# Key products of the next batch behind the last totals of the current one, value turning in front of the first query products

## The chip, the cores and the metric

The kernel runs on one core of a Trainium2 chip. The metric is the device time of one execution in microseconds (us), as the median of several runs. Beside it stands one profiled execution, whose span runs from its first to its last instruction. The engines are TensorE (PE, with its weight loads listed apart as PEld), VectorE (DVE), ScalarE (ACT), GpSimd (POOL) and SyncE (SP, whose queue issues most DMAs).

## The reference

Two stages follow each other. The first is a linear attention with a degree-two sketch; the second is a gated feed-forward block (FFN) over the result.

```python
q, k, v: (4, 4, 1088, 32)       # batch, heads, sequence, head size;  S1, S2: (8, 32)
phi(x)  = outer(S1 x, S2 x)      # 8 x 8 = 64 features for each position
kv  = sum_s phi(k)_s v_s         # 64 x 32 for each batch and head
z   = sum_s phi(k)_s             # 64
out = (phi(q) kv) / (phi(q) z + 1e-6)
x   = out as (4352, 128)         # positions x (heads * head size)
y   = (silu(x w_gate) * (x w_val)) w_out     # d_ff = 1536
```

## The kernel before

Everything is fp32. The 4352 positions are cut into 12 blocks, three for each batch, of 384, 384 and 320 positions (`steps`, `blocks`). The FFN works on one block and one of 12 slices of d_ff at a time. `unit(i, j)` (L519 to L535) does two 128x128 matmuls into two PSUM banks, g and u, then a Silu on ScalarE from g, then on VectorE the product `hj` with u. `down()` (L547) multiplies an earlier `hj` with `wo` and sums twelve of them in the bank `acc`. With the twelfth, `store` turns the block back on VectorE (L575) and issues four output DMAs on SP. `down` runs two units behind (`LAG`). Three PSUM banks, g0 to g2, serve g and u in turn through `bank()`, so g of a unit takes the bank that u of two units earlier had, and waits for that unit's `hj`. The sums of a new block wait in the same way for L575 of the block before.

The attention of batch b+1 is spread over the FFN of batch b. `attention(b)` is a generator; each `next` runs it up to its next `yield`, and the piece's instructions are put behind the unit and the `down` just written. The lists `groups` say behind which units that is. Engines work their instructions in the order written (`manual_schedule`), so this order is the schedule. The pieces of one batch are:

- `turn_k` twice (L260): VectorE transposes the loaded keys `kld` into `kT`; then `load_k(b + 1)` refills `kld` over SP.
- key products (L276): 18 matmuls in two pieces of chunks, (0, 5) into the PSUM tile a and (5, 9) into the tile b. Behind each piece ScalarE copies half of the products to `ka` (L290). `key_features` (L296) then multiplies on VectorE, and `feature_sums` adds up on GpSimd (L453).
- values and sums (L307, L477), 40 matmuls into a, and their copy (L481); `load_v(b + 1)`; the turning of the first queries (L266).
- `turn_kv` (L330): four matmuls that turn values and sums into b, copied to `kvz` on ScalarE (L490).
- three times: query products (L351) into a and b, ScalarE copies `qb` (L365), VectorE products `phq` (L379); then, in a piece of its own, totals (L401) into a or b and `divide` (L422 to L447), five VectorE instructions that write the block's `xT`.

The tiles a and b are two PSUM banks wide each. The attention matmuls use small parts of the array (L276 and L330 128 rows by 64 columns, L307 and L477 128 by 32, L351 32 by 64, L401 64 by 32), while the FFN uses all of it.

The first batch's attention is computed in a start-up stage written out by hand. Then come the FFN units of batch 0, in an order written out (`seq`), with the first pieces of `attention(1)` among the last of them. After these follows a stretch without units, called the drain below: groups of three leftover `down`s alternate with pieces of `attention(1)`. Then the loop at L749 runs batches 1 to 3 with 36 units each, z = 0 to 35; in batches 1 and 2 the pieces of the next attention stand behind the units named in `groups`. Each piece between two FFN matmuls is called an attention group below.

Of the kernel before, what the change touches and what calls it, by code (L numbers as in the profile page):

```python
# [17 lines left out]
def kernel(  # L18
# [29 lines left out]
    P = nc.NUM_PARTITIONS  # L48
    B, H, S, Dh = q.shape
# [5 lines left out]
    NC = (NX + 3) // 4  # L55
# [9 lines left out]
    steps = [(sum(plan[:s]), n) for s, n in enumerate(plan)]  # L65
# [20 lines left out]
    def bank(tag=None):  # L86
        if tag is None:
            tag = free_banks[turn[0] % len(free_banks)]
            turn[0] += 1
        return psum.tile([P, TB], FP32, tag=tag, name="bank")  # L90

    def wide(tag):
        return psum.tile([P, 2, TB], FP32, tag=tag, name=tag)
# [17 lines left out]
    kpieces = ((0, 5), (5, NC))  # L111
# [3 lines left out]
    def load_k(b):  # L115
        nc.sync.dma_start(
            out=kld[:, 0:NX, :], in_=k[b].rearrange("h (pp x) d -> (h pp) x d", pp=32)
        )

    def load_q(b, x0=0, x1=NX):  # L120
        src = q[b].rearrange("h (pp x) d -> (h pp) x d", pp=32)
        nc.sync.dma_start(out=qld[:, x0:x1, :], in_=src[:, x0:x1, :])
# [124 lines left out]
    def run(*gens):  # L247
        for g in gens:
            for _ in g:
                pass  # L250
# [7 lines left out]
    def turn_k(c0, c1):  # L258
        four = "p (a c) d -> p a c d"
        nc.vector.transpose(  # L260
            out=kT[:, c0:c1, :, :].rearrange("p c a t -> p a c t"),
            in_=kld[:].rearrange(four, a=4)[:, :, c0:c1, :],
        )
# [7 lines left out]
    def key_products(ps, c0, c1, aside=False):  # L271


        for c in range(c0, c1):
            for a in (0, 2):
                nc.tensor.matmul(  # L276
                    ps[32 * a : 32 * a + 64, 64 * (c - c0) : 64 * (c - c0) + 64],
                    kT[:, c, a : a + 2, :].rearrange("p a t -> p (a t)"),
                    s12[:].rearrange("p h t r -> p (h t r)"),
                    start=True,  # L280
                    stop=True,
                )
        n = c1 - c0
        ab = ps[:, 0 : 64 * n].rearrange("p (x t r) -> p x t r", t=2, r=R)
        if aside:
            kab = apool.tile([P, n * H, 2, R], FP32, tag="kab", name="kab")
            nc.scalar.copy(kab[:], ab)
            return kab[:, :, 0, :], kab[:, :, 1, :]
        ka = apool.tile([P, n * H, R], FP32, tag="ka%d" % c0, name="ka")
        nc.scalar.copy(ka[:], ab[:, :, 0, :])  # L290
        return ka[:], ab[:, :, 1, :]
# [102 lines left out]
    def totals(n, phq, kvz, nd):  # L394

        w = 32 * n
        for t in (1, 0):
            for h in range(H):
                for half in range(2):
                    r = slice(F * half, F * half + F)  # L400
                    nc.tensor.matmul(  # L401
                        halves(nd[t])[half][32 * h : 32 * h + 32, 0:w],
                        kvz[t][r, 32 * h : 32 * h + 32],
                        phq[r, h, 0:w],
                        start=True,
                        stop=True,
                    )
        return nd

    def side_by_side(tag):  # L410
        both = wide(tag)[:].rearrange("p g (t w) -> p g t w", t=2)
        return both[:, :, 0, :], both[:, :, 1, :]

    def divide(b, x0, n, nd, among=()):


        w = 32 * n
        t0 = S * b + 64 * x0
        dT = apool.tile([P, 2 * XS, 32], FP32, tag="dT", name="dT", bufs=2)
        rc = apool.tile([P, 2 * XS], FP32, tag="rc", name="rc", bufs=2)  # L420
        rd = apool.tile([P, 2 * XS, 32], FP32, tag="rd", name="rd", bufs=2)
        nc.vector.transpose(  # L422
            out=dT[:, 0 : 2 * n, :].rearrange("p (a x) t -> p a x t", a=2),
            in_=nd[1][:, :, 0:w].rearrange("p a (x t) -> p a x t", t=32),
        )
        nc.vector.tensor_scalar_add(rc[:, 0 : 2 * n], dT[:, 0 : 2 * n, 0], 1e-6)
        nc.vector.reciprocal(rc[:, 0 : 2 * n], rc[:, 0 : 2 * n])
        nc.vector.transpose(
            out=rd[:, 0 : 2 * n, :], in_=rc[:, 0 : 2 * n].unsqueeze(2).to_broadcast([P, 2 * n, 32])
        )  # L430
        if among:
            part(*among)
        xs = xT[:, t0 : t0 + 2 * w].rearrange("p (x a t) -> p a x t", a=2, t=32)
        rs = rd[:, 0 : 2 * n, :].rearrange("p (a x) t -> p a x t", a=2)
        flat, deep = "p (x t) -> p x t", "p a (x t) -> p a x t"
        if isinstance(nd[0], list):
            todo = [(xs[:, a], nd[0][a][:, 0:w].rearrange(flat, t=32), rs[:, a]) for a in (0, 1)]
        else:
            todo = [(xs, nd[0][:, :, 0:w].rearrange(deep, t=32), rs)]
        if t0 == blocks[LAST][0]:  # L440

            m = SPLIT // 64
            ys = xT[:, t0 + SPLIT : t0 + BW].rearrange("p (t x a) -> p a x t", a=2, t=32)
            _, num, r = todo.pop()
            todo = [(xs[:, :, 0:m], num[:, :, 0:m], r[:, :, 0:m]), (ys, num[:, :, m:], r[:, :, m:])]
        for x, num, r in todo:
            nc.vector.tensor_tensor(out=x, in0=num, in1=r, op=ALU.mult)  # L447
# [9 lines left out]
        add(s[:, 0, :], s[:, 0, :], rows[:, 8, :])  # L457
        return s[:, 0, :].rearrange("p (h f) -> p h f", h=H)

    def attention(b):  # L460

        for c0, c1 in kpieces:
            turn_k(c0, c1)
            if c1 == NC and b + 1 < B:
                load_k(b + 1)
            yield
        phk = apool.tile([P, NC, H, R, R], FP32, tag="phk", name="phk")
        prods = [key_products(wide(t)[:, 0, :], *c) for t, c in zip("ab", kpieces)]
        key_features(phk, prods[0], *kpieces[0])
        yield  # L470
        key_features(phk, prods[1], *kpieces[1])
        zs = feature_sums(phk)
        yield
        kvp = wide("a")
        key_values(kvp[:, 0, :], phk, 0, NC)
        for h in range(H):
            nc.tensor.matmul(  # L477
                kvp[32 * h : 32 * h + 32, 1, 0:F], ones[:], zs[:, h, :], start=True, stop=True
            )
        kvs = apool.tile([P, 2, F], FP32, tag="kvs", name="kvs")  # L480
        nc.scalar.copy(kvs[:], kvp[:, :, 0:F])  # L481
        if b + 1 < B:
            load_v(b + 1, [nc.sync] * 4)
        turn_q(*steps[0])
        yield
        kvz = apool.tile([P, 2, P], FP32, tag="kvz", name="kvz", bufs=2)
        kzp = wide("b")[:, 0, 0 : 2 * P].rearrange("p (t n) -> p t n", t=2)
        for t in range(2):
            turn_kv(kvs[:, t, :], kzp[:, t, :])
        nc.scalar.copy(kvz[:], kzp)  # L490
        kvz = kvz[:, 0, :], kvz[:, 1, :]
        yield
        tags = "ab"
        for i, (x0, n) in enumerate(steps):
            phq = query_features(n, query_products(x0, n, tags))
            if i + 1 < len(steps):
                turn_q(*steps[i + 1])
            elif b + 1 < B:
                load_q(b + 1)
            yield  # L500
            divide(b, x0, n, totals(n, phq, kvz, side_by_side(tags[0])))
            tags = tags[::-1]
            yield


# [113 lines left out]
    for c in fpieces:  # L619
        turn_k(*c)  # L620
    prods = [
        key_products(bank(t), *c, aside=(c[1] == NC))
        for t, c in zip(("g1", "g2", "acc"), fpieces)
    ]
    phk = apool.tile([P, NC, H, R, R], FP32, tag="phk", name="phk")
    kz, kv = bank("g0")[:, 0 : H * F], wide("b")[:, 0, 0:F]
    n = steps[0][1]
# [13 lines left out]
    kvz = [apool.tile([P, P], FP32, name=x) for x in ("kvz0", "kvz1")]  # L641
# [5 lines left out]
    phq = query_features(n, pss, qbs)  # L647
# [17 lines left out]
    nd = totals(n, phq, kvz, ([bank(t) for t in ("g2", "acc")], side_by_side("a")[0]))  # L665
# [8 lines left out]
    att = attention(1)  # L674
# [4 lines left out]
    phq = query_features(steps[1][1], pss, qbs)  # L679
# [40 lines left out]
    for z, (i, j) in enumerate(seq):  # L720
# [15 lines left out]
        if z in groups:  # L736
            next(att)
    todo.sort()
    while todo:
        for _ in range(3):  # L740
            if todo:
                down()
        next(att, None)
    run(att)

    groups = (0, 1, 3, 4, 8, 11, 14, 17, 20, 23, 26, 29)
    for b in range(1, B):  # L749
        att = attention(b + 1) if b + 1 < B else None  # L750
        for z in range(3 * NCH):
            i, j = z // NCH, z % NCH
            unit(3 * b + ((0, 2, 1)[i] if b == B - 1 else i), j)
            for _ in range(2):
                if len(todo) > LAG:
                    down()
            if att and z in groups:
                next(att)
        if att:
            run(att)  # L760
    ps = wide("a")[:, 0, 0:D]
    for j in range(NCH):
        if todo and j % 4 == 0:
# [39 lines left out]
```

## Time and profile before

| what | value |
|---|---|
| median of 3 runs | 321.84 us (321.78 to 322.18) |
| the profiled execution's own time | 321.65 us |
| its span | 319.9 us |
| TensorE clock granted | 0.999 |
| PE busy | 312.2 us, 98% of the span |
| VectorE busy | 157.8 us, 49% |
| ScalarE busy | 99.0 us, 31% |
| GpSimd busy | 37.6 us, 12% |

The page counts busy time over the whole span. A matmul's end is modelled and its start is recorded, so the distances between starts tell more than the busy time. In an answer of the timeline a row gives the start, the time from the first start to the last end, the engine, the line, the operation with the names of its tiles, the shapes, and a count; an fp32 matmul appears there as two passes, so "x2" is one matmul.

### The profile page before, as it was taken

The numbers are of one execution on the slowest core, as the hardware profiler recorded it, in microseconds if no ns is written. First come the engines' busy times: TensorE is split into PE (matmuls) and PEld (weight loads), VectorE is DVE, ScalarE is ACT, GpSimd is POOL, SyncE is SP. The second block draws the span as 40 slices with busy tenths as digits, with TensorE's granted clock in tenths as the row PEclk, the third lists the DMA queues.
The fourth block names the chain that finished last, engine by engine and source line by source line (L and its number), as shares of the span: only waits on it lengthen the run. The fifth ranks groups of instructions, "written<-read, shape, count | busy, mean of one in ns | idle before, by whom it ended". The sixth has DMA issues, their size and how long they took to land.

```text
span 319.9 us, 5604 instructions
## 1 busy us (share of the span) xinstructions
PE 312.2 (98%) x2300; PEld 193.7 (61%) x2300; DVE 157.8 (49%) x332; ACT 99.0 (31%) x227; POOL 37.6 (12%) x53
## 2 busy tenths in 40 slices
PE   8989999999999999999999999999999999999994
PEld 6545565655556665555666656555667655676664
DVE  4887999442556532554643542354544332323321
ACT  3467755321211322222322222313222222222230
POOL 2324234072000230000000060000000000000000
PEclk9999999999999999999999999999999999999999
DMA  7553490204041201100210100100010100100101
GB/s 206 155 151 100 162 243 2 72 0 97 2 94 27 65 22 50 27 0 2 39 58 0 22 2 0 24 4 2 0 27 0 21 0 2 26 0 0 21 2 25
DMA packets 24665, 13.99 MB, mean 44 GB/s; under 512 B 18368, under 2 KB 22720, under 8 KB 24640
## 3 DMA queue, kind: packets, MB, share of 16 engines
q1 hardware_dynamic: 24000, 13.54, 16.7%
q8 instruction: 18, 0.29, 0.4%
q10 hardware_dynamic: 640, 0.10, 0.2%
q14 instruction: 7, 0.06, 0.1%
HBM read 11.41 MB, written 2.23 MB: 43 GB/s over the span
## 4 chain that ended last, share of the span: by engine, by line
PE 88%; DVE 7%; issue 2%; ACT 1%; POOL 0%; DVEq 0%
PE bank L519 49%; PE bank L547 27%; DVE hj L533 2%; PE a L351 2%; PE a L401 2%; PE b L351 1%; PE bank L197 1%; PE a L307 1%; DVE exp L227 1%; PE a L561 1%; DVE man L231 1%; PE b L401 1%; PE a L276 1%; DVE exp L219 1%; ACT exp L224 1%
## 5 line engine op out<-in xcount | busy, mean ns | idle before, releaser
L533 DVE TENSOR_TENSOR hj<-sg,bank 128x384 f32<-128x384 f32 (+1 forms) x138 | 72.7, 528 | 118.2 <-PE bank L519 117.3
L525 ACT ACTIVATE sg<-bank 128x384 f32<-128x384 f32 (+1 forms) x144 | 67.9, 472 | 162.7 <-PE bank L519 161.9
L519 PE MATMUL bank<-xT,wg 128*128 128x384 f32 (+1 forms) x288 | 113.7, 477 | 1.2 <-POOL wg L235 1.1
L519 PE MATMUL bank<-xT,wv 128*128 128x384 f32 (+1 forms) x288 | 111.5, 469 | 0.5 <-DVE hj L533 0.5
L547 PE MATMUL bank<-hj,wo 128*128 128x384 f32 (+2 forms) x288 | 106.8, 462 | 0.3 <-DVE hj L533 0.2
L519 PEld LDWEIGHTS bank<-xT,wv 128*128 128x128 f32 x288 | 54.4, 190 | 34.5 <-DVE hj L533 2.1
L547 PEld LDWEIGHTS bank<-hj,wo 128*128 128x128 f32 x288 | 53.9, 190 | 33.2 <-issue 2.4
L519 PEld LDWEIGHTS bank<-xT,wg 128*128 128x128 f32 x288 | 52.7, 190 | 32.3 <-issue 3.9
L453 POOL TENSOR_TENSOR zs<-phk 128x1024 f32<-128x1024 f32 x3 | 7.0, 2348 | 115.5 <-PE bank L519 106.0
L379 DVE TENSOR_TENSOR phq<-a,qb 128x384 f32<-128x384 f32 (+1 forms) x11 | 5.8, 531 | 10.7 <-ACT qb L365 10.7
L365 ACT COPY qb<-a 128x384 f32<-128x384 f32 (+1 forms) x11 | 5.1, 460 | 15.1 <-PE b L351 8.6
L351 PE MATMUL a<-qT,sq 32*64 32x192 f32 (+1 forms) x176 | 9.2, 324 | 0.0
L351 PE MATMUL b<-qT,sq 32*64 32x192 f32 (+1 forms) x176 | 9.2, 324 | 0.0
L227 DVE SCALAR_TENSOR_TENSOR exp<-raw,exp 128x384 int32<-128x384 int32 (+2 forms) x14 | 8.6, 618 | 0.9 <-ACT exp L224 0.9
L224 ACT ACTIVATE exp<-exp,rebias 128x384 int32<-128x384 int32 (+3 forms) x15 | 8.2, 550 | 2.7 <-DVE exp L219 2.0
L422 DVE STREAM_TRANSPOSE dT<-a 128x384 f32<-128x384 f32 (+1 forms) x8 | 4.4, 550 | 7.8 <-PE a L401 7.8
L365 ACT COPY qb<-b 128x384 f32<-128x384 f32 (+1 forms) x11 | 5.1, 463 | 9.7 <-PE b L351 6.4
L575 DVE STREAM_TRANSPOSE o<-bank 128x384 f32<-128x384 f32 (+2 forms) x12 | 6.6, 549 | 2.7 <-PE bank L547 2.3
L351 PEld LDWEIGHTS a<-qT,sq 32*64 32x64 f32 x176 | 5.5, 131 | 3.9 <-issue 3.0
L379 DVE TENSOR_TENSOR phq<-b,qb 128x384 f32<-128x384 f32 (+1 forms) x11 | 5.8, 527 | 4.2 <-ACT qb L365 4.2
L231 DVE SCALAR_TENSOR_TENSOR man<-raw,man 128x384 f32<-128x384 uint32 (+2 forms) x14 | 6.9, 493 | 0.0
L225 ACT ACTIVATE man<-man 128x384 f32<-128x384 int32 (+3 forms) x15 | 6.7, 450 | 0.5 <-DVE man L220 0.5
(96 smaller groups left out, 168.9 us busy)
## 6 DMA issues: line engine op xcount, KB each, us to landing
kld<-in_k_dram SPq DMA_DIRECT2D x4, 544.0 KB, 4.1
vld<-in_v_dram SPq DMA_DIRECT2D x12, 144.0 KB, 4.3
qld<-in_q_dram SPq DMA_DIRECT2D x3, 544.0 KB, 3.9
raw<-in_moe_w_out_dram SPq DMA_DIRECT2D x4, 384.0 KB, 5.8
out_dram<-o SPq DMA_DIRECT2D x28, 48.0 KB, 1.9
raw<-in_moe_w_gate_dram SPq DMA_DIRECT2D x3, 384.0 KB, 3.3
raw<-in_moe_w_val_dram SPq DMA_DIRECT2D x3, 384.0 KB, 3.5
out_dram<-o SPq DMA_DIRECT2D x16, 40.0 KB, 1.7
```

Source lines behind the costliest of these rows:

```text
L224: nc.scalar.activation(e[:], e[:], AF.Relu, bias=rebias[: shape[0], :], scale=8.0)
L227: nc.vector.scalar_tensor_tensor(out=e[:], in0=hi, scalar=-(1 << 31), in1=e[:], op0=ALU.bitwise_and, op1=ALU.bitwise_or,)
L231: nc.vector.scalar_tensor_tensor(out=f, in0=lo, scalar=2.0**-52, in1=f, op0=ALU.mult, op1=ALU.add)
L351: nc.tensor.matmul(parts[g][F * half : F * half + F, t, 0:w], sq[r, t, :, :].rearrange("p i j -> p (i j)"), qT[r, x0 : x0 + n, half, :], s ...
L365: nc.scalar.copy(qb[:, :, 0:w], both[:, :, 1, 0:w])
L379: nc.vector.tensor_tensor(out=phq[:, 2 * pr : 2 * pr + 2, 0:w], in0=both[:, :, 0, 0:w], in1=qb[:, :, 0:w], op=ALU.mult,)
L401: nc.tensor.matmul(halves(nd[t])[half][32 * h : 32 * h + 32, 0:w], kvz[t][r, 32 * h : 32 * h + 32], phq[r, h, 0:w], start=True, stop=True,)
L453: add = lambda o, a, b: nc.gpsimd.tensor_tensor(out=o, in0=a, in1=b, op=ALU.add)
L519: nc.tensor.matmul(o[:, 0:n], w[:, j, :], xT[:, t0 : t0 + n], start=True, stop=True)
L525: nc.scalar.activation(sg[:, 0:n], g[:, 0:n], AF.Silu)
L533: nc.vector.tensor_tensor(out=hj[:, 0:n], in0=sg[:, 0:n], in1=u[:, 0:n], op=ALU.mult)
L547: nc.tensor.matmul(acc[i][:, 0:n], wo[:, j, :], hidden[i, j][:, 0:n], start=(j == 0), stop=(j == NCH - 1),)
```

## The change

The keys of the next batch are handled at the end of the current attention. `turn_k` of the first piece stands behind the second `divide`, that of the second piece behind the last query features, followed by `load_k` of the batch after. The key products (`next_keys`) stand right behind the last totals and in front of their `divide`; they now put both pieces into one wide tile, the first piece into its first bank and the second into its second. The generator hands them back with `return`, and the next `attention` starts from them. `attention(1)` still makes its own key products, now into tile b. The `yield` between `turn_kv` and the first query products is gone, so both stand together; the turned values go into one of the three rotating banks in place of b. The first two batches of the loop have the pieces behind other units.

```diff
+    def next_keys(tag):
+        both = wide(tag)
+        return [key_products(both[:, i, :], *c) for i, c in enumerate(kpieces)]
-    def attention(b):
-        for c0, c1 in kpieces:
-            turn_k(c0, c1)
-            if c1 == NC and b + 1 < B:
-                load_k(b + 1)
-            yield
+    def attention(b, prods=None):
+        if prods is None:
+            for c in kpieces:
+                turn_k(*c)
+                yield
+            load_k(b + 1)
+            prods = next_keys("b")
         phk = apool.tile([P, NC, H, R, R], FP32, tag="phk", name="phk")
-        prods = [key_products(wide(t)[:, 0, :], *c) for t, c in zip("ab", kpieces)]
         key_features(phk, prods[0], *kpieces[0])
         yield
...
-        kzp = wide("b")[:, 0, 0 : 2 * P].rearrange("p (t n) -> p t n", t=2)
+        kzp = bank()[:, 0 : 2 * P].rearrange("p (t n) -> p t n", t=2)
...
         kvz = kvz[:, 0, :], kvz[:, 1, :]
-        yield
         tags = "ab"
...
             elif b + 1 < B:
                 load_q(b + 1)
+                turn_k(*kpieces[1])
+                if b + 2 < B:
+                    load_k(b + 2)
             yield
-            divide(b, x0, n, totals(n, phq, kvz, side_by_side(tags[0])))
+            nd = totals(n, phq, kvz, side_by_side(tags[0]))
+            last = i + 1 == len(steps)
+            if last and b + 1 < B:
+                prods = next_keys(tags[1])
+            divide(b, x0, n, nd)
+            if i == 1 and b + 1 < B:
+                turn_k(*kpieces[0])
             tags = tags[::-1]
+            if last:
+                return prods
             yield
...
-    groups = (0, 1, 3, 4, 8, 11, 14, 17, 20, 23, 26, 29)
+    groups = (0, 1, 6, 9, 12, 15, 18, 21, 24)
     for b in range(1, B):
-        att = attention(b + 1) if b + 1 < B else None
+        att = attention(b + 1, keys) if b + 1 < B else None
```

The rest of the diff (`attend`) catches what the generator returns and hands it to the next.

More of the change, by code (lines that the diff above doesn't have):

```diff
@@ L738, with attend @@
     todo.sort()
+    keys = None
+    def attend():
+        nonlocal att, keys
+        try:
+            if att:
+                next(att)
+        except StopIteration as end:
+            att, keys = None, end.value
     while todo:
@@ L742 @@
                 down()
-        next(att, None)
-    run(att)
-    groups = (0, 1, 3, 4, 8, 11, 14, 17, 20, 23, 26, 29)
+        attend()
+    while att:
+        attend()
+    groups = (0, 1, 6, 9, 12, 15, 18, 21, 24)
     for b in range(1, B):
-        att = attention(b + 1) if b + 1 < B else None
+        att = attention(b + 1, keys) if b + 1 < B else None
         for z in range(3 * NCH):
@@ L756 @@
                     down()
[L757 to L760, printed above, removed]
+            if z in groups:
+                attend()
+        while att:
+            attend()
     ps = wide("a")[:, 0, 0:D]
```

## The prediction

> **What bounds the kernel now.** I read the page first, then the timeline of PE group by group, then VectorE and ScalarE at the same places. The page says PE:
>
> ```profile
> PE 312.2 (98%) x2300; PEld 193.7 (61%) x2300; DVE 157.8 (49%) x332; ACT 99.0 (31%) x227; POOL 37.6 (12%) x53
> PE bank L519 49%; PE bank L547 27%; DVE hj L533 2%; PE a L351 2%; PE a L401 2%; PE b L351 1%; PE bank L197 1%; PE a L307 1%; DVE exp L227 1%; PE a L561 1%; DVE man L231 1%; PE b L401 1%; PE a L276 1%; DVE exp L219 1%; ACT exp L224 1%
> ```
>
> No PE wait is listed after 100 us. What PE loses there lies in its starts. PE's timeline around the value turning, and the one place at the start-up where L330 is followed by another small shape:
>
> ```profile
> 122.93 0.81 PE L547 MATMUL bank<-hj,wo 128*128 128x384 f32 x2
> 123.67 0.66 PE L330 MATMUL b<-ident,kvs 128*64 128x128 f32 x8
> 124.25 0.91 PE L519 MATMUL bank<-xT,wg 128*128 128x384 f32 x2
> 125.00 0.81 PE L519 MATMUL bank<-xT,wv 128*128 128x384 f32 x2
> ...
> 12.31 0.44 PE L330 MATMUL bank<-ident,kvs 128*64 128x128 f32 x4 [0.15 <-DVE kvs L659]
> 12.68 0.56 PE L401 MATMUL a<-phq,kvz 64*32 64x192 f32 x16
> ```
>
> A 384-wide FFN matmul takes 0.645 us from start to start (125.00 to 125.65). L547 to L330 takes 0.74, so 0.095 goes on entering; wg to wv takes 0.75, so 0.105 on leaving. Query products (start 130.25 after 129.52, then 131.12 and 131.87) and totals show 0.085 to 0.09 and 0.10. Each attention group thus pays about 0.195 us over its own stretch.
>
> The key group of batch 1, on PE and ScalarE:
>
> ```profile
> 104.60 0.81 PE L547 MATMUL bank<-hj,wo 128*128 128x384 f32 x2
> 105.34 0.80 PE L276 MATMUL a<-s,kT 128*64 128x64 f32 x20
> 105.97 0.64 PE L276 MATMUL b<-s,kT 128*64 128x64 f32 x16
> 106.54 0.91 PE L519 MATMUL bank<-xT,wg 128*128 128x384 f32 x2
> ...
> 106.19 0.29 ACT L290 COPY ka<-a 128x160 f32<-128x160 f32 x1 [1.54 <-PE a L276]
> 106.65 0.27 ACT L290 COPY ka<-b 128x128 f32<-128x128 f32 x1 [0.17 <-PE b L276]
> ```
>
> To be seen: the second piece starts at 105.97, before ScalarE has begun to copy the first. They are separate tiles.
>
> Last, the first totals of batch 2 with VectorE behind them:
>
> ```profile
> 137.12 0.88 PE L401 MATMUL a<-phq,kvz 64*32 64x192 f32 x32
> 139.32 0.81 PE L547 MATMUL bank<-hj,wo 128*128 128x384 f32 x2
> 141.26 0.81 PE L547 MATMUL bank<-hj,wo 128*128 128x384 f32 x2
> ...
> 139.81 0.56 DVE L447 TENSOR_TENSOR xT<-a,rd 128x384 f32<-128x384 f32 x1
> 140.28 0.55 DVE L533 TENSOR_TENSOR hj<-sg,bank 128x384 f32<-128x384 f32 x1
> 155.36 0.58 DVE L575 STREAM_TRANSPOSE o<-bank 128x384 f32<-128x384 f32 x1
> ```
>
> The next hj waits behind divide until 140.28, 3.16 us after the totals began. It costs nothing here, because no store is near.
>
> **What the Trainium skill says.** "TensorEngine Tiling (Array Packing)", Key Properties: "Mode switching requires drain". "TensorE: Matmul & The Clock Gate", Step-by-step, adds that the next weights are loaded while a matmul runs. The trace agrees with both: 0.645 us in a row, 0.095 and 0.105 more at each switch. "PSUM — Partial Sum Buffer", the section on bank collisions, says that accesses of two engines to different banks run clean. By that the two banks of one wide tile need no order between them; what the program waits for is another question.
>
> **The change part by part.** Sums are against the profiled execution (span 319.9, own time 321.65); the median of 321.84 moves with it.
>
> *Fewer groups.* Turning and first query products merge for attention(1), (2) and (3); last totals and next keys merge for attention(1) and (2). That is five merges. All matmuls stay. A merge drops one leaving (0.105) and one entering (0.09) if the switch between two small shapes costs what one from small to full does. At the start-up four passes of L330 give way to L401 after 0.37; eight passes give way to wg after 0.58, less four passes (two pairs, 0.11 each) 0.36. So it does. 5 x 0.195 = 0.98 us gained.
>
> *The drain.* Before, the third query products (92.01) lost time: their second half started at 92.78, when divide had freed b (L447 there at 92.08 for 0.56). The group took 1.47 us where the same group at 156.87 takes 0.75. In the new order the three downs ahead of it are two of 384 and one of 320, not three of 320: 2 x 0.107 = 0.21 more work under the same wait. 0.21 gained. Behind divide VectorE now has turn_k (0.84) and L575 (0.58), then phq; that ends some 5.5 us after the totals began, and the next totals come at 5.9. Free.
>
> *The key products' new wait.* In the built program's list of waits, the first matmul of the second piece waits for ScalarE's count of the first piece's ka copy, in all three key groups: both pieces are in one tile. PE is in order, so the second piece and every FFN matmul behind it stand. By the rows: the first piece's last pass is at 105.92; the copy runs 106.19 to 106.48; a waiting engine follows 0.03 to 0.05 later (phk at 106.51); so the second piece starts at 106.53, not 105.97. That is 0.56, and 0.05 for a weight load without cover: 0.61. From both sides: 0 if the copy were early, 0.75 if refilling the array costs as at the entry. I take 0.61, as PE has nothing else to do meanwhile: 3 x 0.61 = 1.83 us lost.
>
> *Totals against stores.* The groups now put the first totals at z=12. Block j=11's down is at z=13, its store L575 behind hj of z=13, and the next block's first down at z=14 waits for L575. With T the totals' start: hj runs from T+3.16, L575 from T+3.63 (0.47 later, as back to back elsewhere) to T+4.21; PE wants the bank at T+4.14 (141.26 less 137.12). With 0.05 of notice and 0.105 of uncovered weight load it goes on at T+4.37: 0.23 lost, in batches 1 and 2. At z=24 of batch 2 the same happens with 320-wide units, where the last totals have no keys behind them: hj from T+2.85 (165.51 less 162.66), L575 to T+3.84, PE at T+3.61: 0.39. In batch 1 the keys' own delay gives VectorE room. Sum 0.85 us. From both sides: 0 if L575 starts earlier, 1.3 if hj is late too.
>
> *Moves that should be free.* turn_k (0.84 and 0.67) goes behind divide and phq. At z=18 hj then ends at T+3.16+0.81+0.55 = T+4.52, and g two units later needs it at T+4.79: 0.2 of slack after notice. Without that, some 0.2 once. key_features (1.49, 1.21) at z=0 and 1 leave hj 0.4 us before its bank is wanted (102.85 against 103.31). GpSimd's sums have 9.7 us instead of 7.7. load_k and load_q go over SP in the order load_q, load_k; stores queue behind them, and kld lands in 4.1 us against many units' time. The rotating bank for kvz costs one 0.37 copy under 0.87 of query products; it is free before a unit wants it.
>
> Sum: -0.98 -0.21 +1.83 +0.85 = +1.49 us; span 321.4, median 323.3.
>
> **Rivals.**
>
> 1. *The stores find room:* merges, drain and key wait as above, no loss at L575. +0.64, so 322.5. For it: the margin is 0.07 to 0.25 us before notice. Against: all terms are read from rows.
>
> 2. *The key wait costs nothing* (the side not slower): the copy's release reaches PE without a gap. -0.98 -0.21 +0.85 = -0.34, so 321.5. It decides once the wait is under 0.33 us per key group, since then the sum is within 0.65. For it: the banks are separate. Against: the wait is in the program and ScalarE starts only 0.27 after the last pass.
>
> 3. *VectorE becomes the bound at the new bursts:* hj late at z=0, 1 and 18 as well, about five stops of 0.2: 324.3. For it: slacks of 0.2 to 0.4. Against: VectorE idles 1.38 before most hj.
>
> 4. *Merged groups run into each other* and save 0.7 each: -3.5 -0.21 +1.83 +0.85 = -1.0, so 320.8. Against it stands the start-up row.
>
> **How the numbers follow.** Within 0.2% (0.65 us, about what a measurement can tell) is 321.2 to 322.5. The likeliest case has 0.57 at 323.3, its own range 322.8 to 323.8. Rival 1 has 0.18, half of it inside the band; rival 2 0.10, mostly inside; rival 3 0.11; rival 4 0.04, faster. Faster 0.06, same 0.17, slower 0.77. The range 322.3 to 324.3 leaves out rivals 2 and 4 and the edges of the others.
>
> **What would show it.** Right: L276 rows in two stretches 0.6 us apart, PE waiting for ka L290 three times; waits of L563 (L547 of before) on L591 (L575) near z=14 and z=24; L330 to L351 about 0.2 shorter than two groups. Wrong: L276's second piece follows within 0.1 us, no stop at the new block's first down, or hj waits in PE's list instead.

## The result and the profile after

The changed kernel takes 323.38 us (median of 4 runs, 323.09 to 323.73) against 321.96 us for the kernel before in the same comparison. The ratio is 1.0044, with a 95% interval of 1.0027 to 1.0061. It is slower by 1.42 us; the forecast was 1.49 us, at 323.3.

The page of the changed kernel, its span, busy times and chain by line:

```profile
span 321.9 us, 5610 instructions
...
PE 311.6 (97%) x2300; PEld 193.4 (60%) x2300; DVE 156.7 (49%) x332; ACT 98.9 (31%) x227; POOL 37.7 (12%) x53
...
PE bank L535 48%; PE bank L563 27%; DVE hj L549 2%; PE a L401 2%; PE a L351 2%; PE b L276 1%; DMA kld<-in_k_dram 1%; PE b L351 1%; PE a L307 1%; DVE exp L227 1%; PE a L577 1%; DVE man L231 1%; PE b L401 1%; PE bank L330 1%; DVE exp L219 1%
```

PE has the same 2300 matmuls and is still the bound, but its busy share is a point lower: holes, stretches in which PE stands still, have come in. In this kernel the FFN lines are L535 (L519 before) and L563 (L547), hj is L549 (L533), the store's turning L591 (L575). The list of waits says how long an engine stood idle for which other one: microseconds in total, how many times, and the longest. PE's list has one new entry behind the start-up:

```profile
PE b L276 <- ACT ka L290: 1.2, 3, 0.4
```

That is 1.2 us in three waits. It is too little: the list counts from the modelled end of the last matmul. The starts show the whole loss. The first key group on PE, and ScalarE beside it:

```profile
59.97 0.80 PE L276 MATMUL b<-s,kT 128*64 128x64 f32 x20
61.16 0.69 PE L276 MATMUL b<-s,kT 128*64 128x64 f32 x16 [0.39 <-ACT ka L290]
61.77 0.91 PE L535 MATMUL bank<-xT,wg 128*128 128x384 f32 x2
...
60.82 0.29 ACT L290 COPY ka<-b 128x160 f32<-128x160 f32 x1 [1.54 <-PE b L276]
```

The second piece starts 1.19 us after the first, where it was 0.63 (105.34 to 105.97); the copy ends at 61.11 and PE goes on at 61.16. The whole group, from its first start to wg's, takes 1.80 us instead of 1.20.

A merged group: the turning and the first query products of `attention(2)`, beside the FFN of batch 1.

```profile
120.94 0.66 PE L330 MATMUL bank<-ident,kvs 128*64 128x128 f32 x8
121.53 0.39 PE L351 MATMUL a<-qT,sq 32*64 32x192 f32 x4
...
122.39 0.91 PE L535 MATMUL bank<-xT,wg 128*128 128x384 f32 x2
```

L330 to L351 takes 0.59, against 0.58 from L330 to wg before (123.67 to 124.25), so the switch itself got no cheaper. The merged group takes 1.45 (120.94 to 122.39), as long as the two groups before together (0.58 and 0.87). What is gone is one leaving and one entering.

In the drain the third query products stopped for a bank that a division was still reading. Their two halves, before and then in the changed kernel:

```profile
92.01 0.77 PE L351 MATMUL a<-qT,sq 32*64 32x160 f32 x16
92.78 0.77 PE L351 MATMUL b<-qT,sq 32*64 32x160 f32 x16
...
91.34 0.77 PE L351 MATMUL a<-qT,sq 32*64 32x160 f32 x16
91.90 0.77 PE L351 MATMUL b<-qT,sq 32*64 32x160 f32 x16
92.60 1.88 PE L563 MATMUL bank<-hj,wo 128*128 128x320 f32 x6
```

The second half starts 0.56 after the first instead of 0.77, and the group takes 1.26 instead of 1.47.

The first totals and the store, PE and then VectorE:

```profile
131.89 0.81 PE L535 MATMUL bank<-xT,wv 128*128 128x384 f32 x2
132.65 0.91 PE L563 MATMUL bank<-hj,wo 128*128 128x384 f32 x2
133.40 0.81 PE L535 MATMUL bank<-xT,wg 128*128 128x384 f32 x2
...
131.56 0.55 DVE L549 TENSOR_TENSOR hj<-sg,bank 128x384 f32<-128x384 f32 x1
132.02 0.58 DVE L591 STREAM_TRANSPOSE o<-bank 128x384 f32<-128x384 f32 x1
```

wv to L563 takes 0.76 instead of 0.645, and L563 to wg 0.75: 0.22 us lost in all. PE starts 0.05 after L591's end at 132.60. PE's list of waits does not show this stop at all, since the modelled end of wv, 132.70, covers it. The same stop comes again at 208.53 (0.22) and, with 320-wide units, at 235.40 (0.37). The list of the weight loads does show all three, and what ended them:

```profile
PEld bank L563 <- DVE o L591: 1.7, 3, 0.6
```

The kernel before has no such entry for its store. The 1.7 us are idle time of the weight loads; PE itself lost 0.81.

One more thing separates the two profiles. The first down product starts later in the changed kernel, although nothing ahead of it was changed:

```profile
51.52 0.89 PE L547 MATMUL bank<-hj,wo 128*128 128x384 f32 x2 [0.21 <-DVE hj L533]
...
52.05 0.88 PE L563 MATMUL bank<-hj,wo 128*128 128x384 f32 x2 [0.22 <-DVE hj L549]
```

Behind it 268.4 us (319.9 less 51.52) stand against 269.85. That is 1.45 us more; the other 0.53 of the 2.0 us between the spans is start-up. For the experiments I give both the median and this rest of the span, counted from the start of the first down product, which leaves the start-up out.

### The profile page after: what moved, and what is told of

Read it like the earlier page. It is cut to its first block, busy times and chain, and to the rows that moved or that the text cites. A ratio compares the mean times of both kernels' runs of the same rounds, so it can differ in the third digit from the quotient of the medians.

```text
span 321.9 us, 5610 instructions
## 1 busy us (share of the span) xinstructions
PE 311.6 (97%) x2300; PEld 193.4 (60%) x2300; DVE 156.7 (49%) x332; ACT 98.9 (31%) x227; POOL 37.7 (12%) x53
## 4 chain that ended last, share of the span: by engine, by line
PE 85%; DVE 8%; issue 2%; ACT 2%; DMA 1%; POOL 0%; SPq 0%; DVEq 0%
PE bank L535 48%; PE bank L563 27%; DVE hj L549 2%; PE a L401 2%; PE a L351 2%; PE b L276 1%; DMA kld<-in_k_dram 1%; PE b L351 1%; PE a L307 1%; DVE exp L227 1%; PE a L577 1%; DVE man L231 1%; PE b L401 1%; PE bank L330 1%; DVE exp L219 1%
## 5 line engine op out<-in xcount | busy, mean ns | idle before, releaser
L549 DVE TENSOR_TENSOR hj<-sg,bank 128x384 f32<-128x384 f32 (+1 forms) x138 | 72.5, 528 | 120.4 <-PE bank L535 119.7
L535 PE MATMUL bank<-xT,wg 128*128 128x384 f32 (+1 forms) x288 | 113.3, 475 | 1.6 <-POOL wg L235 1.1
L535 PE MATMUL bank<-xT,wv 128*128 128x384 f32 (+1 forms) x288 | 111.6, 469 | 0.5 <-DVE hj L549 0.5
L563 PE MATMUL bank<-hj,wo 128*128 128x384 f32 (+2 forms) x288 | 106.9, 463 | 0.4 <-DVE hj L549 0.2
L535 PEld LDWEIGHTS bank<-xT,wv 128*128 128x128 f32 x288 | 54.4, 190 | 34.4 <-DVE hj L549 2.1
L563 PEld LDWEIGHTS bank<-hj,wo 128*128 128x128 f32 x288 | 53.7, 190 | 34.1 <-issue 1.9
L535 PEld LDWEIGHTS bank<-xT,wg 128*128 128x128 f32 x288 | 53.1, 190 | 32.7 <-issue 3.3
L591 DVE STREAM_TRANSPOSE o<-bank 128x384 f32<-128x384 f32 (+2 forms) x12 | 6.5, 544 | 6.0 <-PE bank L563 5.8
L351 PE MATMUL a<-qT,sq 32*64 32x192 f32 (+1 forms) x176 | 9.2, 324 | 0.0
L351 PE MATMUL b<-qT,sq 32*64 32x192 f32 (+1 forms) x176 | 9.2, 324 | 0.0
L296 DVE TENSOR_TENSOR phk<-ka,b 128x1280 f32<-128x1280 f32 (+1 forms) x6 | 8.1, 1344 | 2.1 <-ACT ka L290 2.1
L351 PEld LDWEIGHTS a<-qT,sq 32*64 32x64 f32 x176 | 5.5, 131 | 3.0 <-PE bank L535 1.6
```

What stands on the lines that cost most here:

```text
L296: engine.tensor_tensor(out=phk[:, c0:c1, :, :, :].rearrange("p c h i j -> p (c h) i j"), in0=ka.unsqueeze(3).to_broadcast([P, n, R, R]), i ...
L351: nc.tensor.matmul(parts[g][F * half : F * half + F, t, 0:w], sq[r, t, :, :].rearrange("p i j -> p (i j)"), qT[r, x0 : x0 + n, half, :], s ...
L535: nc.tensor.matmul(o[:, 0:n], w[:, j, :], xT[:, t0 : t0 + n], start=True, stop=True)
L549: nc.vector.tensor_tensor(out=hj[:, 0:n], in0=sg[:, 0:n], in1=u[:, 0:n], op=ALU.mult)
L563: nc.tensor.matmul(acc[i][:, 0:n], wo[:, j, :], hidden[i, j][:, 0:n], start=(j == 0), stop=(j == NCH - 1),)
```

## The experiments

The theory is the sum in the prediction: five merges -0.98, drain -0.21, key wait +1.83, stores +0.85. Two rivals stand against it here. One says that VectorE's bursts in general cost the time; the other, that the start-up makes up 0.5 us of it.

**Undo the key wait.** All 18 products first, then both copies; everything else as changed. `key_copy` is the copy to `ka`, taken out of `key_products`.

```diff
-        return [key_products(both[:, i, :], *c) for i, c in enumerate(kpieces)]
+        made = [key_products(both[:, i, :], *c, copy=False) for i, c in enumerate(kpieces)]
+        return [key_copy(*m) for m in made]
```

> The changed kernel with one thing undone: ScalarE copies the first half of the key products only after all 18 products have been written, so the second half of the products waits for no copy. Theory of the prediction (five merges -0.98, drain -0.21, key wait +1.83, stores +0.85): the key wait falls away, 1.83 us under the changed kernel, which is 0.3 us under the kernel before; the L276 rows of each key group follow each other without the 0.6 us hole; the stops at z=14 and z=24 stay. Rival 'VectorE': if late hj products made most of the loss, this gives at most 0.5 us. Rival 'start-up': if 0.5 of the 1.42 us lies in the start-up, which in the profile of the changed kernel ends 0.52 us later, the kernel lands 0.2 us over the kernel before instead.

Measured: 321.49 us against 321.82, ratio 0.9988 (0.998 to 0.9996); rest of the span 268.0 us, 1.86 under the changed kernel. The group on PE's timeline:

```profile
59.45 1.27 PE L276 MATMUL b<-s,kT 128*64 128x64 f32 x36
60.65 0.91 PE L541 MATMUL bank<-xT,wg 128*128 128x384 f32 x2
```

The hole is gone and the group is back at 1.20 us. With this one wait taken away the change is a gain of 0.33 us. The theory stands; the rival on VectorE, whose work is the same here, is out as the main cause, since by it this edit should have given 0.5 us at most.

**Undo the collision with the stores.** The groups from the first totals on stand one unit later.

```diff
-    groups = (0, 1, 6, 9, 12, 15, 18, 21, 24)
+    groups = (0, 1, 6, 9, 13, 16, 19, 22, 25)
```

> The changed kernel with the attention groups from the first totals on one unit later (13, 16, 19, 22, 25 in place of 12, 15, 18, 21, 24), so that the store of a finished block stands ahead of the division on VectorE. Theory: the three stops at the new block's first down go (0.22, 0.22 and 0.37 us in the profile), 0.8 us under the changed kernel, 0.65 over the kernel before. Rival 'VectorE': the load on VectorE is the same, so if bursts of it are what costs, the time stays within 0.2 of the changed kernel.

Measured: rest of the span 269.0 us, 0.84 under the changed kernel, as expected, and all three stops are gone from PE's starts. The median, 323.0 us, was a miss: 1.18 over the kernel before (ratio 1.0037, 1.0025 to 1.0049) where 0.65 was expected. The profiled execution is itself the median of the five. Of the 1.35 us by which its span exceeds that of the kernel before, 0.60 lie behind the first down product and 0.75 ahead of it, which starts at 52.27. So the start-up accounts for the miss in that execution; the other four have no such record, and whether this program starts up later as a rule was not tested. The place right behind the first totals of batch 2:

```profile
131.35 0.91 PE L535 MATMUL bank<-xT,wg 128*128 128x384 f32 x2
132.10 0.81 PE L535 MATMUL bank<-xT,wv 128*128 128x384 f32 x2
132.74 0.81 PE L563 MATMUL bank<-hj,wo 128*128 128x384 f32 x2
133.39 0.81 PE L535 MATMUL bank<-xT,wg 128*128 128x384 f32 x2
134.03 0.81 PE L535 MATMUL bank<-xT,wv 128*128 128x384 f32 x2
```

Steps of 0.645 throughout behind the first. Division and store on VectorE still follow each other, but the store now goes first:

```profile
130.65 0.58 DVE L591 STREAM_TRANSPOSE o<-bank 128x384 f32<-128x384 f32 x1
131.53 0.58 DVE L422 STREAM_TRANSPOSE dT<-a 128x384 f32<-128x384 f32 x1 [0.30 <-PE a L401]
```

**Undo both.** The two edits together.

> Both edits together: copies after all products, and the totals one unit later. Theory: only the gains are left, five merges and the drain, -1.19 us against the kernel before, some 320.8. Rival 'start-up': 0.5 less than that, -0.7. Rival 'VectorE': later pieces push the bursts together at the batch's end, nothing gained over the first edit alone.

Measured: 320.77 us, ratio 0.997 (0.9959 to 0.9981), 1.05 us under the kernel before; rest of the span 267.2, which is 1.19 under the kernel before. The gains alone were put at 1.19.

**The key wait alone.** The kernel before, with both pieces in one wide tile.

```diff
-        prods = [key_products(wide(t)[:, 0, :], *c) for t, c in zip("ab", kpieces)]
+        one = wide("b")
+        prods = [key_products(one[:, i, :], *c) for i, c in enumerate(kpieces)]
```

> The kernel before with one edit: both pieces of the key products go into one wide tile (one bank each) instead of two tiles. Nothing is merged or moved. Theory: the second piece waits for ScalarE's copy of the first, 0.61 us in each of three key groups, +1.83 us on the kernel before. Rival 'key wait free': under +0.3 us, since PE has other work in its queue.

Measured: 324.01 us, 2.19 over the kernel before (ratio 1.007, 1.0058 to 1.0082); rest of the span 270.2, 1.81 over. Batch 2's key group, with the copy on ScalarE:

```profile
106.41 0.80 PE L276 MATMUL b<-s,kT 128*64 128x64 f32 x20
107.61 0.69 PE L276 MATMUL b<-s,kT 128*64 128x64 f32 x16 [0.39 <-ACT ka L290]
108.22 0.91 PE L520 MATMUL bank<-xT,wg 128*128 128x384 f32 x2
...
107.26 0.29 ACT L290 COPY ka<-b 128x160 f32<-128x160 f32 x1 [1.54 <-PE b L276]
```

1.20 us between the pieces again, with nothing merged or moved. The wait comes with the shared tile, and it alone costs more than the whole change lost.

**The turning alone.** The kernel before, with only the merge of the turning and the first query products: three merges, and with them the drain's new order.

```diff
-        kzp = wide("b")[:, 0, 0 : 2 * P].rearrange("p (t n) -> p t n", t=2)
+        kzp = bank()[:, 0 : 2 * P].rearrange("p (t n) -> p t n", t=2)
...
-        yield
-    groups = (0, 1, 3, 4, 8, 11, 14, 17, 20, 23, 26, 29)
+    groups = (0, 1, 3, 4, 8, 14, 17, 20, 23, 26, 29)
```

> The kernel before with one part of the change: turning of values and sums in front of the first query products, with the turned values in a rotating bank; the keys stay where they were. Theory: three merges of 0.198 and, as the drain's last queries get the same three downs ahead, 0.21 there: -0.80 us, 321.0; from the first down on 267.6 us instead of 268.4. Rival 'merged groups run into each other': 0.7 a merge, -2.3. Rival 'bank': the extra use of a rotating bank delays the next units, and nothing is gained.

Measured: 321.21 us against 321.89, 0.68 under it (ratio 0.9975, 0.9965 to 0.9985); rest of the span 267.6, 0.80 under the kernel before. A merge is worth what the switches at its seam cost; the rivals that merged groups run into each other, or that the rotating bank eats the gain, are out.

**The collision alone.** The kernel before, with its groups at other units.

```diff
-    groups = (0, 1, 3, 4, 8, 11, 14, 17, 20, 23, 26, 29)
+    groups = (0, 1, 2, 3, 7, 8, 9, 12, 15, 18, 21, 24)
```

> The kernel before with other places for the attention groups alone, so that its first and last totals come at z=12 and z=24 as in the changed kernel (0, 1, 2, 3, 7, 8, 9, 12, 15, 18, 21, 24). Nothing is merged. Theory: the new block's first down waits for the store that waits behind the division: 0.22 at z=14 and 0.38 near z=26, in batches 1 and 2 both, as here no key products stand behind the last totals: +1.2 us, and the PE starts show the stops there. Rival: place does not matter, within 0.2 of the kernel before.

Measured: 323.07 us, ratio 1.0033 (1.0021 to 1.0045), 1.18 over the kernel before; rest of the span 269.6, 1.15 over. There are four stops, two in each batch. The second of batch 1, PE and VectorE:

```profile
157.84 0.70 PE L519 MATMUL bank<-xT,wv 128*128 128x320 f32 x2
158.64 0.81 PE L547 MATMUL bank<-hj,wo 128*128 128x320 f32 x2
159.28 0.70 PE L519 MATMUL bank<-xT,wg 128*128 128x320 f32 x2
...
158.01 0.58 DVE L575 STREAM_TRANSPOSE o<-bank 128x384 f32<-128x384 f32 x1
```

0.80 and 0.64 between starts where 0.54 is usual: 0.37 us. Place alone makes this loss, and the list of the weight loads has four waits for L575.

**The changed kernel again**, measured beside the turning alone, the collision alone and the version that follows.

> The changed kernel again, to stand beside the other kernels of this call. Theory: from the first down product on (51.5 us before, 52.1 in the first profile of the changed kernel) the rest of the span is 269.85 us as in the first profile, within 0.1; what differs between runs lies ahead of that point. Rival 'start-up': the start-up of the changed kernel is longer by the same 0.5 us again.

Measured: 323.3 us, ratio 1.004 (1.0029 to 1.0052); rest of the span 269.83; the first down product at 51.67, against 52.05 in the first profile of the same program. The rest repeats within 0.02 us; the start-up does not. So the rival that the change lengthens it by 0.5 falls, and the median, 1.41 over the kernel before, agrees with the rest's 1.45.

**A version that beats both.** Both losses undone, and something done about two more stops, which the kernel before had too: in the drain, four downs instead of three stand between totals and the next query products.

```diff
-    while todo:
-        for _ in range(3):
-            if todo:
-                down()
+    for n in (3, 4, 3, 4, 3, 6):
+        for _ in range(n):
+            down()
         attend()
```

> The kernel with both losses undone (copies after all products, totals one unit later), and in the drain four downs instead of three between totals and the next query products, two fewer at the end. Theory: the second and third query products of the drain stop no longer for the bank that the division reads (1.68 and 1.62 us in their groups against 1.28 and 1.17 without a stop), 0.85 us under that kernel, 266.4 from the first down on, 2.0 us under the kernel before. Rival: the stops move to the totals behind, whose products are now later, and under 0.3 us is gained.

Measured: 319.87 us, ratio 0.9934 (0.9922 to 0.9945), 2.0 us under the kernel before; rest of the span 266.4, 0.78 under the version with both undone, where 0.85 was expected. The stops had been the second and third query products' waits for the division that reads their bank. The third, PE with VectorE's last step of the division:

```profile
90.99 0.36 PE L356 MATMUL a<-qT,sq 32*64 32x160 f32 x4
91.12 0.36 PE L356 MATMUL b<-qT,sq 32*64 32x160 f32 x4
...
90.41 0.56 DVE L452 TENSOR_TENSOR xT<-b,rd 128x384 f32<-128x384 f32 x1
```

With one more down ahead, the division ends at 90.97, before b is wanted. The two groups take 0.94 and 0.83 where each took 1.26. The same groups without a stop take 0.86 and 0.76 elsewhere, so 0.08 is left in each; what it is was not looked into.

## Why the prediction was right

| step of the prediction | forecast, us | shown by |
|---|---|---|
| five merges | -0.98 | turning alone: three merges and the drain -0.80, forecast -0.80 |
| drain | -0.21 | its group 1.26 instead of 1.47; both undone: five merges and the drain -1.19, forecast -1.19 |
| key products' new wait | +1.83 | alone +1.81; undone -1.86 |
| totals against stores | +0.85 | undone -0.84; at other places alone +1.15, forecast +1.2 |
| sum | +1.49 | rest of the span +1.45; median +1.42 |

The experiments' figures are of the rest of the span. Each term came out by itself, so the sum is right by its parts and not because errors cancelled. With the sizes read from the starts the account closes: five merges -0.98 (the 1.19 of both undone, less the drain), drain -0.21, three key waits +1.83, three stops +0.81, together the 1.45 of the rest.

*Fewer groups.* The switch between two small shapes does cost what one from small to full costs; the one start-up row that the step rested on was enough. The Trainium skill, "TensorEngine Tiling (Array Packing)", Key Properties, says that a change of tiling mode drains TensorE. The trace agrees in so far as L330 to the next small shape took 0.59, and to the full array 0.58.

*Key wait.* Each of the three waits was put at 0.61 and measured 0.60 to 0.61. Its price is the round trip: 0.27 from the last product's start to the copy's, 0.29 the copy, 0.05 back to PE, less the 0.05 to the next pass that was there anyway, and 0.05 for a weight load that could not be made ahead. The last of these the prediction took from no row. The second piece, up to the start of wg, took 0.61 (61.16 to 61.77) instead of 0.57 (105.97 to 106.54), which bears it out to within 0.01. The Trainium skill, "PSUM — Partial Sum Buffer", in its section on bank collisions, says that accesses of two engines to different banks run clean. The trace before agrees: ScalarE read tile a from 106.19 to 106.48 while PE wrote tile b, and the group took the same 1.20 us as in the run with both copies behind all products. So the wait belongs to the program's order within one tile, not to the banks.

*Stores.* 0.23, 0.23 and 0.39 were forecast; 0.22, 0.22 and 0.37 measured. One detail lies elsewhere: the prediction let PE start again only at T+4.37, with the uncovered weight load ahead of the start. PE started at T+4.26 (132.65, with totals at 128.39), and the 0.105 came behind it. The sum is the same.

*Moves called free.* No PE wait for turn_k, the key features, GpSimd's sums or a load stands behind the start-up in any of the profiles of the changed kernel. The starts, which show short stops too, have none at z=0, 1 and 18, so that rival did not occur.

What the prediction had no term for is the start-up: the profiled execution came out 2.0 us longer, not 1.49, and its span 321.9, not 321.4. The last section follows the start-up as far as the profiles go; no experiment tested it.

## What to carry to other kernels

Where one engine is busy 98%, a change's worth is the sum of start-to-start distances on that engine: price each seam between unlike instructions from a row, and look there for stops, because PE's list of waits counts only from modelled ends and missed these 0.81 us. The list of the weight loads had them. Putting two things into one tile added an order here that two tiles did not have; write all of the producer's work before the first reader, or keep two tiles. When work is regrouped, check what it now stands in front of in each in-order queue: a division with 2.1 us of VectorE's work ahead of a store cost 0.2 to 0.4 us, and behind the store, one unit later, nothing.

## What the runs showed that was not expected

The start-up varies by itself. The first down product starts between 51.52 and 52.27 us in ten profiles, 51.67 and 52.05 for one and the same program, and programs with the change and without it are mixed in that range (kernel before 51.52, turning alone 52.06, key wait alone 51.99, collision alone 51.60).

Most of the spread is there by the first value products of the start-up (L307). Before, and in the first profile of the changed kernel:

```profile
10.34 0.90 PE L307 MATMUL b<-phk,vld 128*32 128x64 f32 x48
...
10.92 0.88 PE L307 MATMUL b<-phk,vld 128*32 128x64 f32 x48 [0.31 <-issue]
```

They start 0.58 later. In the changed kernel's profile the weight load ahead of them is listed with a wait of 0.8 us for the loads of the values (`vld`), and in the kernel before with none for them. From there to the first down product both take about the same, 41.2 and 41.1 us. The four profiles with the latest first down product (51.99 to 52.27) are the four with the latest first value products (10.89 to 11.14), and in each the weight load waited 0.7 to 1.0 us for `vld`. In the other six these products start between 10.27 and 10.56, and one has such a wait, of 0.6. Why the values land earlier in one execution than in another stays open. Behind the first down product the same program repeats within 0.02 us.
